# Splitting two weight matrices into high and low parts: POOL casts and VectorE subtracts, with a ring of four tiles

## The chip, the cores and the metric

The kernel runs on one core of a Trainium2 chip. A core has five engines that matter here: TensorE (PE, matrix products), VectorE (DVE), ScalarE (ACT), GpSimd (POOL) and SyncE (SP, which issues DMAs). Each takes its instructions in the order in which they are written, and they wait for each other by semaphores. The metric is the device time of one execution in microseconds, lower is better. Three runs before the change took 979.77, 981.46 and 983.20 us, median 981.46.

## The reference

The output is a block-causal attention followed by a gated MLP, all in float32:

```python
# q, k, v: (8 batches, 8 heads, 576 positions, 64 dims)
scores = (1 / sqrt(64)) * q @ k.T          # per batch and head
scores = where(block_i >= block_j, scores, -1e9)   # blocks of 64 positions
attn = softmax(scores)                     # with 1e-9 added to the sum
x = (attn @ v)                             # heads side by side: (4608, 512)
a = x @ w1                                 # (512, 1024)
b = x @ w2                                 # (512, 1024)
h = a * b @ w3                             # (1024, 1024)
out = h @ w_out                            # (1024, 512)
```

## The kernel before, in words

Two heads form a pair; the 8 batches have 4 pairs each, 32 in all. Pairs 0 to 3 (batch 0) are the early stage, the other 28 the long stage. In the long stage every pair's attention is interleaved with the MLP of the batch before. TensorE's order is written out by hand: `PLAN` and `EARLY_PLAN` (lines 46 to 62) list the steps of a pair as letters, S for a tile of scores, M for a step of the next pair's row maxima, V for a product with V, C for a step of weight preparation, W for a step of the product w3 @ w_out, which is computed once. The other engines' instructions are ordered by a scheduler that knows their dependencies; in the early stage the steps other than C and W have priority.

To keep float32 accuracy, the MLP multiplies split operands: w1 = w1h + w1l, w2 = w2h + w2l, where the high part is the value rounded to the type that TensorE takes in one pass (`fp32r`), and the low part is what is left. `gen_moe` uses w1h, w1l, w2h and w2l, `gen_prod` makes w3 @ w_out and splits it into `wh` and `wl`.

The weights arrive as raw 64-bit words. `load_w` (line 138) rebuilds one tile of 128x512 values, here called a unit, in five steps:

- SP loads the raw words into `wraw`, a ring of five buffers (L143).
- ScalarE writes the upper bits into `wy` (L150), a ring of buffers, and a byte of the lower bits into `wbits` (L151).
- POOL writes another byte into `wbits` (L152). There are two `wbits` tiles, used in turn.
- VectorE assembles `wy` and `wbits` to the value (L153): for w3 and w_out straight into their tiles `w3` and `wo`, for w1 and w2 back into `wy`.

For w1 and w2 `load_rows` (line 156) then writes the high part (L161) and the low part (L162) of each unit; a step C does two units, 16 units in all. A `wy` buffer is free again when the last reader of its value is done.

Around this, in the early stage: ScalarE's exp (`pe`, L273) takes each tile of scores (`s`, L265) from one of two buffers, and TensorE can't begin the next tile of scores until it has. VectorE's reductions (`m`, L196) take the row maxima out of the products `mx` (L192), also two buffers. Small DMAs on ScalarE's queue (L218, L232, L233) place the maxima (`ms`) and copies of Q and K into `qk`. L235 subtracts the high part of Q and K, L166 casts.

Of the kernel before, what the change touches and what calls it, by code (L numbers as in the profile page):

```python
# [8 lines left out]
F32 = mybir.dt.float32  # L9
# [6 lines left out]
ALU = mybir.AluOpType  # L16
# [3 lines left out]
P = 128  # L20
# [47 lines left out]
def block_causal_attention__then__gated_mlp_kernel(ctx, tc, qkv, consts, ident_in, w1, w2, w3t, wout, out_t):  # L68
    nc = tc.nc
# [47 lines left out]
    tl = {}  # L117
# [19 lines left out]

    def load_w(dst, src):
        t = tl["early"].tile([P, 1024], I32, tag="wraw", name="wraw", bufs=5)
        y = tl["early"].tile([P, 512], F32, tag="wy", name="wy", bufs=3)  # L140
        bits = tl["bits"][tl["unit"] % 2]
        tl["unit"] += 1
        nc.sync.dma_start(out=t, in_=src)  # L143
        high = t.rearrange("p (c two) -> p c two", two=2)[:, :, 1]
        byte = t.bitcast(U8).rearrange("p (c e) -> p c e", e=8)
        if dst is None:
            dst = y
        low = bits.bitcast(U8).rearrange("p (c e) -> p c e", e=4)[:, :, 0]
        top = bits.bitcast(F8).rearrange("p (c e) -> p c e", e=4)[:, :, 3]
        nc.scalar.mul(out=y, in_=high.bitcast(F32), mul=2.0**-112)  # L150
        nc.scalar.activation(out=top, in_=byte[:, :, 7], func=AF.Copy, bias=127.5 * 2.0**-60, scale=-(2.0**-60), saturate=False)  # L151
        nc.gpsimd.tensor_scalar(out=low, in0=byte[:, :, 3], scalar1=1.0 / 32, scalar2=-31.0 / 64, op0=ALU.mult, op1=ALU.add)  # L152
        nc.vector.scalar_tensor_tensor(out=dst.bitcast(I32), in0=y.bitcast(I32), scalar=3, in1=bits, op0=ALU.logical_shift_left, op1=ALU.bitwise_or)  # L153
        return y

    def load_rows(dst_h, dst_l, src):
        for c in range(NC):
            for h in range(2):
                cs = slice(h * 512, (h + 1) * 512)
                val = load_w(None, src[2 * c + h])  # L160
                nc.vector.tensor_copy(dst_h[:, c, cs], val)  # L161
                nc.gpsimd.tensor_tensor(out=dst_l[:, c, cs], in0=val, in1=dst_h[:, c, cs], op=ALU.subtract)  # L162
            yield

    def cast(n, dst, src, act):
# [208 lines left out]
    def gen_w(wp):  # L374
        def rows(u):
            for k in range(2 * u, 2 * u + 2):
                load_w(tl["wo"][:, k, :], wout[k])

        def w3(m):
            assert done[0] >= m - 1  # L380
            t3_of[m] = wp.tile([P, NF, P], F32, tag="w3", name="w3", bufs=2)
            for h in range(2):
                load_w(t3_of[m][:, 4 * h : 4 * h + 4, :].rearrange("p k f -> p (k f)"), w3t[2 * m + h])

        def split(dst_h, dst_l, src):
            g = load_rows(dst_h, dst_l, src)
            return lambda _: next(g)

        one, two = split(w1h, w1l, w1), split(w2h, w2l, w2)
        for u in range(4):  # L390
            rows(u)
            yield
        m, rest = 0, [one] * 4 + [two] * 4
        while m < NF or rest:
            if m < NF and done[0] >= m - 1 and (m < 2 or len(rest) <= 9 - m or not rest):
                w3(m)
                m += 1
            else:
                rest.pop(0)(None)
            yield  # L400
# [188 lines left out]
```

## Time and profile before

| what | value |
|---|---|
| median of three runs | 981.46 us (979.77 to 983.20) |
| the profiled execution | 982.55 us, span 980.6 us |
| PE busy | 941.6 us, 96% of the span |
| DVE busy | 692.4 us, 71% |
| ACT busy | 557.3 us, 57% |
| POOL busy | 629.6 us, 64% |
| mean granted clock of TensorE | 0.993 of full speed |

The span is from the first to the last instruction in the trace; the execution's own time is a little longer. The busy shares are means over the early and the long stage, so they have to be read stage by stage. In the rows below, `L162` is line 162 of the kernel, `w2l<-wy,w2h` says that w2l is written from wy and w2h, and a row of a timeline gives start, length, engine, line, operation, the number of instructions merged into it (`x2`) and, in brackets, how long the engine was idle before it and for whom it waited.

### The profile page before, as it was taken

The page shows a single profiled execution, that of the slowest core. Times are in us where ns is not written, and L with a number is a line of the kernel's source. Part 1 is how long each engine was busy: PE and PEld are TensorE (multiplying, and loading weights), DVE is VectorE, ACT ScalarE, POOL GpSimd, SP SyncE. Part 2 cuts the span into 40 slices and gives each one's busy share as a digit, 9 for nine tenths or more (in the row PEclk, how much of TensorE's full clock was granted, in tenths as well). Part 3 has the DMA queues.
Part 4 walks back from the last instruction along what each step waited for, and adds up shares of the span by engine and source line. Part 5 has one row for each costly group of instructions (what it writes and reads, how often), then busy time and mean ns, then how long its engine had stood idle before and what let it go on. Part 6 is the DMA issues. An engine that isn't in the chain of part 4 may idle for free.

```text
span 980.6 us, 18312 instructions
## 1 busy us (share of the span) xinstructions
PE 941.6 (96%) x6594; PEld 879.1 (90%) x6624; DVE 692.4 (71%) x1230; ACT 557.3 (57%) x1451; POOL 629.6 (64%) x605
## 2 busy tenths in 40 slices
PE   3788989999999999999999999999999999999998
PEld 1444449999999999999999999999999999999998
DVE  6776857777777778878777777788787877774100
ACT  6776635656556665566565556655656555553221
POOL 6786737767676767677676767676776767673211
PEclk9999989999999999999999999999999999999999
DMA  8967502222222221222222221211222222100000
GB/s 294 304 198 221 163 19 62 63 75 63 87 63 75 63 87 41 66 69 65 73 66 83 64 80 57 88 54 53 69 72 66 69 81 63 50 13 25 7 19 25
DMA packets 31303, 79.81 MB, mean 81 GB/s; under 512 B 5356, under 2 KB 13676, under 8 KB 31212
## 3 DMA queue, kind: packets, MB, share of 16 engines
q1 hardware_dynamic: 29788, 76.26, 25.4%
q10 hardware_dynamic: 1424, 2.38, 1.0%
q8 instruction: 52, 0.85, 0.4%
q14 instruction: 39, 0.32, 0.1%
HBM read 50.76 MB, written 9.44 MB: 61 GB/s over the span
## 4 chain that ended last, share of the span: by engine, by line
PE 88%; ACT 3%; DVE 3%; POOL 3%; issue 2%; DMA 1%; ACTq 0%; SPq 0%; POOLq 0%; DVEq 0%
PE ab L426 42%; PE o L442 21%; PE s L265 9%; PE x L320 9%; PE mx L192 3%; PE w L407 2%; POOL wbits L152 1%; ACT wbits L151 1%; DMA wraw<-in_w 1%; ACT wy L150 1%; POOL w2l L162 1%; PE x L304 1%; DVE m L196 1%; ACT pe L273 1%; DVE qk L166 0%
## 5 line engine op out<-in xcount | busy, mean ns | idle before, releaser
L286 POOL TENSOR_TENSOR rsum<-rsum,p 128x448 f32<-128x448 f32 x224 | 186.1, 831 | 87.1 <-ACT p L280 76.8
L435 POOL TENSOR_TENSOR gl<-g,gh 128x288 fp32r<-128x288 f32 x128 | 114.5, 895 | 121.5 <-ACT gh L434 121.5
L283 DVE TENSOR_TENSOR pl<-p,ph 128x448 fp32r<-128x448 f32 x168 | 149.1, 901 | 60.1 <-ACT ph L281 59.2
L265 PE MATMUL s<-qk 128*128 128x288 f32 (+4 forms) x768 | 157.3, 314 | 16.3 <-ACT pe L273 10.8
L235 POOL TENSOR_TENSOR qk<-raw,qk 64x1152 fp32r<-64x1152 f32 x58 | 154.9, 2670 | 9.1 <-issue 6.1
L426 PE MATMUL ab<-xh,w2h 128*128 128x288 f32 x512 | 153.8, 300 | 0.0
L442 PE MATMUL o<-gh,wh 128*128 128x288 f32 x512 | 153.6, 300 | 0.0
L426 PE MATMUL ab<-xh,w1h 128*128 128x288 f32 x512 | 151.1, 295 | 0.0
L426 PE MATMUL ab<-xl,w2h 128*128 128x288 f32 x512 | 151.0, 295 | 0.0
L426 PE MATMUL ab<-xl,w1h 128*128 128x288 f32 x512 | 151.0, 295 | 0.0
L426 PE MATMUL ab<-xh,w1l 128*128 128x288 f32 x512 | 151.0, 295 | 0.0
L442 PE MATMUL o<-gh,wl 128*128 128x288 f32 x512 | 150.9, 295 | 0.0
L426 PE MATMUL ab<-xh,w2l 128*128 128x288 f32 x512 | 150.9, 295 | 0.0
L442 PE MATMUL o<-gl,wh 128*128 128x288 f32 x512 | 150.8, 295 | 0.0
L265 PEld LDWEIGHTS s<-qk 128*128 128x128 f32 (+1 forms) x768 | 116.9, 183 | 28.5 <-ACT pe L273 16.1
L434 ACT CAST gh<-g 128x288 fp32r<-128x288 f32 x128 | 55.4, 433 | 142.8 <-DVE g L433 142.7
L281 ACT ACTIVATE ph<-s 128x288 fp32r<-128x288 f32 x336 | 131.4, 393 | 0.0
L196 DVE TENSOR_REDUCE m<-mx 128x1 f32<-128x64 f32 (+3 forms) x320 | 128.3, 446 | 3.0 <-PE mx L192 0.8
L280 ACT ACTIVATE p<-s 128x448 f32<-128x448 f32 x224 | 85.5, 382 | 51.5 <-PE s L265 50.7
L283 DVE TENSOR_TENSOR pl<-rsum,ph 128x288 fp32r<-128x288 f32 x112 | 75.7, 677 | 49.2 <-ACT ph L281 45.4
L320 PE MATMUL x<-ph,vs 128*128 128x128 f32 x336 | 110.4, 329 | 0.0
L433 DVE TENSOR_TENSOR g<-ab,a 128x288 f32<-128x288 f32 x128 | 56.5, 441 | 69.5 <-PE ab L426 68.6
(76 smaller groups left out, 2182.4 us busy)
## 6 DMA issues: line engine op xcount, KB each, us to landing
raw<-in_qkv SPq DMA_DIRECT2D x31, 896.0 KB
qk<-qk SPq DMA_DIRECT2D x108, 144.0 KB
out_t<-o SPq DMA_DIRECT2D x64, 144.0 KB
wraw<-in_w3t SPq DMA_DIRECT2D x16, 512.0 KB
wraw<-in_w SPq DMA_DIRECT2D x16, 512.0 KB
wraw<-in_wout SPq DMA_DIRECT2D x8, 512.0 KB
qk<-qk ACTq DMA_DIRECT2D x16, 144.0 KB
qk<-ms SPq DMA_DIRECT2D x54, 2.2 KB
```

Of the source, the lines that this page charges most:

```text
L196: nc.vector.reduce_max(m[:, col : col + 1], sc, axis=AX.X)
L235: (nc.gpsimd if "late" in tl or n * j else nc.vector).tensor_tensor(out=qk[j][o, 2:4], in0=rqk[o], in1=qk[j][o, 0:2], op=ALU.subtract)
L265: nc.tensor.matmul(t[ks, at : at + q1 - q0], qk[j][:, k, kr], qk[j][:, q, q0:q1], start=(s == 0), stop=(s == 1))
L280: nc.scalar.activation(p32, t[ks, at : at + w], AF.Exp, scale=SCALE)
L281: nc.scalar.activation(ph[ks, o : o + w], t[ks, at : at + w], AF.Exp, scale=SCALE)
L283: nc.vector.tensor_tensor(out=low, in0=p32, in1=ph[ks, o : o + w], op=ALU.subtract)
L286: nc.gpsimd.tensor_tensor(out=r, in0=r, in1=p32, op=ALU.add)
L320: nc.tensor.matmul(xps[:, to : to + w], v[:, c, :], pr[:, a : a + w], start=(u < 2 and s == 0), stop=(u in (0, len(PV) - 1) and s == len(p ...
L426: nc.tensor.matmul(t[:, 0:HALF], l[:, c, fs], r, start=(c == 0 and s == 0), stop=(c == NC - 1 and s == 2))
L433: nc.vector.tensor_tensor(out=g32, in0=acc[1][:, 0:HALF], in1=a32, op=ALU.mult)
L435: nc.gpsimd.tensor_tensor(out=gl[:, f, :], in0=g32, in1=gh[:, f, :], op=ALU.subtract)
L442: nc.tensor.matmul(t[:, 0:HALF], l[:, f, es], r[:, f, :], start=(f == 0 and s == 0), stop=(f == NF - 1 and s == 2))
```

## The change

POOL writes the high parts of w1 and w2 (L161) and VectorE the low parts (L162); before it was the reverse. The ring of `wy` has four buffers where it had three.

```diff
     def load_w(dst, src):
         t = tl["early"].tile([P, 1024], I32, tag="wraw", name="wraw", bufs=5)
-        y = tl["early"].tile([P, 512], F32, tag="wy", name="wy", bufs=3)
+        y = tl["early"].tile([P, 512], F32, tag="wy", name="wy", bufs=4)
...
                 val = load_w(None, src[2 * c + h])
-                nc.vector.tensor_copy(dst_h[:, c, cs], val)
-                nc.gpsimd.tensor_tensor(out=dst_l[:, c, cs], in0=val, in1=dst_h[:, c, cs], op=ALU.subtract)
+                nc.gpsimd.tensor_copy(dst_h[:, c, cs], val)
+                nc.vector.tensor_tensor(out=dst_l[:, c, cs], in0=val, in1=dst_h[:, c, cs], op=ALU.subtract)
```

The scheduler orders the engines anew; TensorE's order stays. Three places show how. Numbers behind a name tell tiles apart: `wy_932` and `wraw_931` belong to one unit, and units follow each other with rising numbers.

VectorE in pair 3, while the units 881 to 995 of w2 are made; before:

```order
L153 SCALAR_TENSOR_TENSOR wy_890<-wy_890,wbits1_110 128x512
L196 TENSOR_REDUCE m4_914<-mx4_1_926 128x1
L161 CAST w2h_88<-wy_890 128x512
L153 SCALAR_TENSOR_TENSOR wy_932<-wy_932,wbits0_109 128x512
L153 SCALAR_TENSOR_TENSOR wy_941<-wy_941,wbits1_110 128x512
L161 CAST w2h_88<-wy_932 128x512
L161 CAST w2h_88<-wy_941 128x512
L196 TENSOR_REDUCE m4_914<-mx4_2_956 128x1
L166 CAST qk0_86<-raw4_831 64x1152
L196 TENSOR_REDUCE m4_914<-mx4_2_956 128x1
L153 SCALAR_TENSOR_TENSOR wy_995<-wy_995,wbits0_109 128x512
```

The same stretch of VectorE after the change:

```order
L162 TENSOR_TENSOR w2l_89<-wy_890,w2h_88 128x512
L196 TENSOR_REDUCE m4_914<-mx4_1_926 128x1
L153 SCALAR_TENSOR_TENSOR wy_932<-wy_932,wbits0_109 128x512
L153 SCALAR_TENSOR_TENSOR wy_941<-wy_941,wbits1_110 128x512
L166 CAST qk0_86<-raw4_831 64x1152
L162 TENSOR_TENSOR w2l_89<-wy_932,w2h_88 128x512
L162 TENSOR_TENSOR w2l_89<-wy_941,w2h_88 128x512
L196 TENSOR_REDUCE m4_914<-mx4_2_956 128x1 x2
L153 SCALAR_TENSOR_TENSOR wy_995<-wy_995,wbits0_109 128x512
```

Both reductions of `mx4_2` now stand behind the subtractions of the units 932 and 941, and the cast of Q and K (L166) stands between those units' assemblies and their subtractions.

ScalarE at the end of pair 3's first head and the start of its second (`pe3_1`); before:

```order
L151 ACTIVATE wbits1_110<-wraw_1003 128x512
L150 ACTIVATE wy_1004<-wraw_1003 128x512
L232 DMA qk0_86<-qk0_86 64x576
L233 DMA qk0_86<-qk0_86 64x576
L150 ACTIVATE wy_1036<-wraw_1035 128x512
L151 ACTIVATE wbits0_109<-wraw_1035 128x512
L150 ACTIVATE wy_1043<-wraw_1042 128x512
L151 ACTIVATE wbits1_110<-wraw_1042 128x512
L273 ACTIVATE pe3_1_979<-s3_1_985 128x288
```

ScalarE there after the change:

```order
L151 ACTIVATE wbits1_110<-wraw_1003 128x512
L232 DMA qk0_86<-qk0_86 64x576
L233 DMA qk0_86<-qk0_86 64x576
L150 ACTIVATE wy_1036<-wraw_1035 128x512
L150 ACTIVATE wy_1043<-wraw_1042 128x512
L151 ACTIVATE wbits0_109<-wraw_1035 128x512
L151 ACTIVATE wbits1_110<-wraw_1042 128x512
L273 ACTIVATE pe3_1_979<-s3_1_985 128x288
```

`wy_1004` has moved further to the front, and the two `wy` of the units 1036 and 1043 stand together ahead of their `wbits`; the exp is still behind all four.

ScalarE at the same point of pair 2; before:

```order
L151 ACTIVATE wbits0_109<-wraw_793 128x512
L244 COPY ve0_154<-raw3_606 128x5x64
L150 ACTIVATE wy_801<-wraw_800 128x512
L273 ACTIVATE pe2_1_738<-s2_1_744 128x288
L273 ACTIVATE pe2_1_738<-s2_1_748 128x288
```

And after the change:

```order
L151 ACTIVATE wbits0_109<-wraw_793 128x512
L150 ACTIVATE wy_801<-wraw_800 128x512
L244 COPY ve0_154<-raw3_606 128x5x64
L273 ACTIVATE pe2_1_738<-s2_1_744 128x288
L273 ACTIVATE pe2_1_738<-s2_1_748 128x288
```

The copy of V (L244) and `wy_801` have changed places. Elsewhere POOL's order around these units is now cast, `wbits`, cast, `wbits`; on SP's queue the load of pair 4's Q, K and V stands ahead of one load of w2 that it followed before; on ScalarE's queue in pair 0 the DMA L232 stands behind two exps and two copies that followed it before; and in pair 2 one `wy` (unit 890) stands ahead of the DMA L218.

## Rows read from the trace of the kernel before

**Rows 1.** Busy time of each engine by stage (stretch: length, busy, instructions, clock, DMA).

```profile
20.00:149.30 129.30, 108.65 (x361) 58.35 (x365) 89.08 (x142) 82.74 (x166) 84.62 (x68) 0.95 0.58 180
...
149.30:980.60 831.30, 828.09 (x6220) 818.75 (x6245) 590.26 (x1068) 461.90 (x1266) 531.93 (x518) 1.00 0.21 61
```

**Rows 2.** Who waited for whom, 0 to 150 us (total us, times, longest).

```profile
PE s L265 <- ACT pe L273: 10.8, 8, 3.6
```

**Rows 3.** Lines 161, 162, 411, 0 to 150 us (ns minimum/median/maximum, start).

```profile
L161 DVE CAST w1h<-wy x8: 409/702/1383, 45.2 to 83.9; 128x512 fp32r<-128x512 f32 x8
...
L162 POOL TENSOR_TENSOR w2l<-wy,w2h x8: 1261/1581/2382, 90.5 to 125.8; 128x512 fp32r<-128x512 f32 x8
...
  ACT wy L150: 18.1, 12
...
L411 DVE TENSOR_TENSOR wl<-w,wh x8: 675/690/693, 52.1 to 149.6; 128x512 fp32r<-128x512 f32 x8
```

**Rows 4.** TensorE's timeline, 0 to 150 us.

```profile
43.60 0.63 PE L265 MATMUL s<-qk 128*128 128x288 f32 x3 [3.81 <-DMA qk<-ms]
...
59.88 0.68 PE L265 MATMUL s<-qk 128*128 128x448 f32 x2 [1.12 <-ACT pe L273]
...
63.74 0.56 PE L265 MATMUL s<-qk 128*128 128x192 f32 x4 [1.02 <-ACT pe L273]
...
69.23 0.95 PE L304 MATMUL x<-pe,ve 128*128 128x192 f32 x4 [0.76 <-ACT pe L273]
...
92.85 1.11 PE L265 MATMUL s<-qk 128*128 128x448 f32 x2 [3.00 <-ACT pe L273]
...
121.22 0.38 PE L192 MATMUL mx<-kb,qd 128*128 128x192 bf16 x2 [2.12 <-DVE m L196]
...
121.96 1.88 PE L407 MATMUL w<-wo,w 128*128 128x512 f32 x4
...
127.49 1.12 PE L265 MATMUL s<-qk 128*128 128x448 f32 x2 [3.65 <-ACT pe L273]
```

**Rows 5.** ScalarE's timeline, 0 to 150 us.

```profile
125.86 0.67 ACT L150 ACTIVATE wy<-wraw 128x512 f32<-128x512 f32 x1 [2.56 <-POOL w2l L162]
...
126.43 0.76 ACT L151 ACTIVATE wbits<-wraw 128x512 fp8e4<-128x512 uint8 x1
```

**Rows 6.** TensorE by slices of 2 us (length, busy, instructions, clock, DMA).

```profile
92.00:94.00 2.00, 1.15 (x5) 0.68 0.72 193
...
94.00:96.00 2.00, 2.00 (x6) 0.50 0.46 80
...
126.00:128.00 2.00, 0.51 (x1) 0.72 0.00 0
...
128.00:130.00 2.00, 2.00 (x7) 0.50 0.00 0
...
132.00:134.00 2.00, 2.00 (x7) 0.58 0.00 0
```

**Rows 7.** Groups of instructions, 0 to 160 us (count, busy us, mean ns, idle before).

```profile
L161 DVE CAST w2h<-wy 128x512 fp32r<-128x512 f32 x8 | 6.9, 882 | 0.0
...
L153 DVE SCALAR_TENSOR_TENSOR wy<-wy,wbits 128x512 int32<-128x512 int32 x16 | 13.9, 889 | 5.6 <-ACT wbits L151 5.5
...
L229 POOL CAST qk<-raw 64x576 fp32r<-64x576 f32 x1 | 0.7, 659 | 0.3 <-DMA raw<-in_qkv 0.3
...
L113 POOL CAST qk<-cst 64x576 fp32r<-64x576 f32 x4 | 4.6, 1147 | 1.9 <-DMA cst<-in_consts 1.7
```

**Rows 8.** VectorE's timeline, 0 to 150 us.

```profile
87.11 1.82 DVE L153 SCALAR_TENSOR_TENSOR wy<-wy,wbits 128x512 int32<-128x512 int32 x2
...
114.21 2.87 DVE L153 SCALAR_TENSOR_TENSOR wy<-wy,wbits 128x512 int32<-128x512 int32 x2
...
118.95 1.68 DVE L166 CAST qk<-raw 64x1152 fp32r<-64x1152 f32 x1
...
120.56 0.61 DVE L196 TENSOR_REDUCE m<-mx 128x1 f32<-128x448 f32 x1
```

## The prediction

> **What bounds the kernel now.** I read the span by stage first: up to 149.3 us the weights are prepared beside the first four pairs of heads, after it comes the long stage of attention and MLP. There TensorE is busy 828.09 of 831.30 us, so nothing that VectorE or POOL does there can be seen in the time; between 20 and 149.3 us it is busy 108.65 of 129.30 us, at a mean clock of 0.95 [rows 1]. Those 20.65 idle us, and what the lowered clock costs, are all that this change can reach (before 20 us no tile of w1 or w2 is handled).
>
> Next I read who waits there. TensorE's scores wait 10.8 us for ScalarE's exp. The exp waits for nothing of its own: ScalarE takes its work in order, and in that order stand the `wy` instructions (the first step of rebuilding a weight tile), which waited 18.1 us, 12 times, for POOL's subtractions of w1l and w2l [rows 2, 3]. A buffer of the `wy` ring is free when POOL has subtracted the tile three units back, and POOL needs a median 1.58 us for one [rows 3]. So the chain is: POOL's subtraction, ScalarE's `wy`, the exp queued behind it, TensorE.
>
> TensorE's timeline gives each such place its price [rows 4]. In pair 1: 1.12 us before the scores at 59.88, 1.02 at 63.74, 0.76 before the product with V at 69.23, together 2.90. In pair 2: 3.00 at 92.85. In pair 3: 2.12 at 121.22, where a reduction on VectorE is late, and 3.65 at 127.49. One more, 3.81 at 43.60, waits for a small DMA. ScalarE's timeline shows the last link before the longest: a `wy` at 125.86 after 2.56 us of waiting for POOL, and behind it `wbits` and the exp [rows 5].
>
> Both long gaps are also followed by a slow clock [rows 6]. Around 94 us the granted clock is 0.50 (1.2 GHz) where it was 1.00 (2.4 GHz) before the gap; half of the busy 1.15 and 2.00 us is lost, 1.6 us. After 126 us the busy 0.51, 2.00, 2.00 (two such slices, one shown) and 2.00 us at 0.58 lose 0.25 + 1.0 + 1.0 + 0.84 = 3.1 us. After the gap of 2.12 us alone the clock stayed at 1.00 (the matmuls that follow it took their usual time, and the 0.72 slice is the first low one).
>
> **The change part by part.**
>
> *POOL.* It loses 16 subtractions at a median of 1.58 us and gets 16 casts. POOL's casts in the trace are smaller: 64x576 in 0.659 us on the quick end, 1.147 us as a mean where VectorE works beside it [rows 7]. Scaled to 512 columns that is 0.59 to 1.02 us; I take 0.8, between the two. So POOL works about 16 x 0.8 = 12.5 us less. It is not on TensorE's path by itself, and this counts only through the waits above.
>
> *VectorE.* It loses 16 casts (mean 0.88 us for w2, 0.41 at best, 1.38 at worst) and gets 16 subtractions with both inputs in SBUF. The nearest rows: the subtraction of the same 128x512 with one input in the accumulators, 0.69; the 128x512 step with two tensor inputs that rebuilds the tile, mean 0.889 [rows 3, 7]. Lower end 0.68, upper end 0.69 plus the longest stretch that a cast suffered (1.38 - 0.41 = 0.97), 1.66. I take 0.89, the row of the same shape with two inputs: against a cast's 0.88 VectorE's load stays where it is.
>
> *The ring.* A `wy` now waits for the tile four units back, that is for the whole step before last, and its last reader is VectorE. In the order this reader stands ahead of the two assemblies of the next step, so ScalarE's `wy` no longer ends the chain. What is late next is `wbits`, which has two buffers as before and waits for VectorE's assembly two units back.
>
> *The added wait.* Each VectorE subtraction waits for POOL's cast of the same tile. Behind it on VectorE stand the row-maximum reductions that free the buffers of TensorE's `mx` products. Mostly the scheduler has put reductions or casts between an assembly and its subtraction, and POOL's order is cast, `wbits`, cast, `wbits`, so one POOL instruction of 0.8 to 1.0 us lies between.
>
> *Moves without a price.* In pair 0 one DMA (L232) on ScalarE's queue goes behind two exps and two copies, about 2 us, while its scores at 43.60 wait for a later one. On SP's queue the load of pair 4's Q, K and V passes one w2 tile; if that cover failed, the tile's two steps would be late by that one load. Reductions and exps in pair 0 move by one `wy`, worth up to 0.6 us, but the wait at 43.60 is for a DMA behind them, so I count none.
>
> Now the places, in the times of before.
> Pair 1: all three gaps were exps behind a `wy` that waited for POOL. The order leaves only waits on assemblies, which were done by then: 2.90 falls to 0.4, saving 2.5.
> Pair 2: the exp behind the gap now waits for `wbits`, that is for two assemblies on VectorE that ended by 88.9 [rows 8], then one `wy` (0.67) and a copy of V: about 90. 3.00 falls to 0.5, saving 2.5, and the clock stays up, 1.6.
> Pair 3, first gap: before, VectorE needed from 114.21 to 121.17 for two assemblies (2.87 with a wait for ScalarE in them), two casts, a cast of Q and K (1.68) and two reductions [rows 8]. After, the same stretch is 2 x 0.89 + 1.68 + 2 x 0.89 + 0.8 = 6.0, ending at 120.2 instead of 121.17: saving 0.9.
> Pair 3, second gap: after that reduction come two assemblies (to 122.0); from the start of the last `wbits` at 126.43 to the scores at 127.49 it took 1.1 us before, so TensorE resumes at 123.1 to 123.2; the four matmuls in front (1.88 us from 121.96, now 0.9 earlier) end at 122.9. Resuming at 123.2 instead of 127.49 saves 4.3, of which 0.9 is already counted, so 3.4; and the clock, 3.1.
> Together 2.5 + 2.5 + 1.6 + 0.9 + 3.4 + 3.1 = 14.0. Against it: one `wy` (0.67, counted 0.6) now stands ahead of the small DMA for the scores of pair 3, whose twin in pair 1 was waited for at 43.60, and I allow 0.9, one subtraction's length, for those that wait for a cast in pair 2. That leaves 12.5. The profiled execution took 982.55, so 970.05; it lay 1.09 above the median of the runs shown, which by itself would give 969.0. I forecast 969.5.
>
> One rule speaks against the exchange. The row: the subtraction with one input in the accumulators always took 0.675 to 0.693, while casts in SBUF went from 0.41 to 1.38 [rows 3]. The Trainium skill, "SBUF — State Buffer", section "Who interferes with whom", says that a VectorE instruction with two SBUF inputs contends with a GpSimd instruction that reads SBUF, and that the loser blocks for the other's whole length. The rows agree; by it every new subtraction can be held by a whole POOL instruction, as the casts were. That is the slow rival below.
>
> **The rivals.**
> 1. *One long gap remains.* The `wbits` ring of two makes ScalarE wait for VectorE, and if subtractions take 1.2 us rather than 0.89, four of them in pair 3 bring the first gap back to 2.4 and leave the clock to fall once. Then the 3.1 and about 2.4 more are not gained: 12.5 - 5.5 = 7.0, 975.5. For it: from 114.21 to 121.17 VectorE goes from one row to the next almost without idle time [rows 8]. Against it: over 20 to 149.3 us it works 89.08 of 129.30 [rows 1], and its load does not grow.
> 2. *The wait only changes its place.* ScalarE's 18.1 us become VectorE's waits for casts, and the reductions are late by as much as the exps were. 14.0 spread over the seven steps of w1 and w2 that lie beside the gaps (of eight) is 2.0 us a step; with that much added on VectorE nothing is gained: 981. Against it: POOL has 12.5 us more time.
> 3. *Slower.* Each subtraction is held by a POOL instruction (1.66 - 0.88 = 0.78, twice a step), and each first subtraction waits for a cast behind a `wbits` (1.0 + 1.02 less the second assembly 0.89, so about 1.1, and 0.4 for the second): 3.1 a step, seven steps, 21.7 against 14.0 saved: 7.7 slower, 990. It decides from 2.0 us a step on. For it: the rule above, and VectorE's order is fixed. Against it: the scheduler put other work between, and casts are half as long as subtractions on POOL.
>
> **How the numbers follow.** Forecast 0.63 (its own range 965 to 973), rival 1 0.20 (975.5), rival 2 0.10 (981), rival 3 0.07 (990). 0.3% of 981.46 is 2.9 us, about what a measurement of this kernel can tell from no change: faster means under 978.5. That gives 0.83 faster, 0.10 the same, 0.07 slower. The range 964 to 979 takes in the forecast and rival 1, and leaves the other two and gains above 17 us outside.
>
> **What would show it.** Right: in the profile after, `wy` waits for the subtraction's line for less than 3 us in total; the gaps of 3.00 and 3.65 are under 1 us; the granted clock is 1.00 in the slices after them; VectorE's subtractions have a mean near 0.9 and POOL's casts near 0.8; the long stage begins near 137 and still takes 831 us. Wrong: subtractions above 1.3, VectorE's reductions waiting behind casts with TensorE's `mx` products late by more than 2 us, a clock of 0.50 after 60 us, or a new long wait for the small DMA in front of the scores.

## The result, and the profile after

The changed kernel takes 970.76 us (median of 6 runs, 968.63 to 974.43), against 981.42 for the kernel before (6 runs). The ratio is 0.9888, with a 95% interval of 0.9869 to 0.9908: 10.7 us faster, and 1.3 us above the forecast of 969.5. Run again with the last experiments, it gave 971.94 and 0.9903 (0.9878 to 0.9927).

The profiled execution took 970.15 us, its span is 968.3 us. The view of busy time by stage, with the border moved to where the long stage now begins (length, busy time of PE, PEld, DVE, ACT, POOL, clock, DMA share, GB/s), answers to [rows 1]:

```profile
20.00:137.15 117.15, 105.90 (x364) 57.88 (x365) 89.81 (x142) 81.35 (x165) 72.57 (x68) 0.97 0.64 198
137.15:968.30 831.15, 828.00 (x6247) 818.75 (x6245) 589.45 (x1068) 461.86 (x1266) 531.56 (x518) 1.00 0.21 61
```

The long stage is what it was, 831.15 us after 831.30. The early stage is 12.15 us shorter; VectorE's load there hardly moved (89.81 after 89.08), POOL's fell by 12.05.

Who waited for whom, 0 to 150 us, all engines (total us, times, longest), answers to [rows 2] and to the waits of `wy` in [rows 3]:

```profile
PE s L265 <- ACT pe L273: 3.6, 5, 1.4
...
ACT wy L150 <- DVE w2l L162: 2.8, 4, 1.5
...
DVE w2l L162 <- POOL w2h L161: 2.7, 2, 1.3
...
DVE w1l L162 <- POOL w1h L161: 1.0, 2, 0.5
ACT wy L150 <- DVE w1l L162: 1.0, 1, 1.0
```

The first step `wy` waited 18.1 us for POOL's subtractions and now waits 3.8 for VectorE's, in 5 places where there were 12; the prediction had asked for less than 3. TensorE's waits for an exp fell from 10.8 us to 3.6. The price, VectorE waiting for POOL's casts, is 3.7 us.

The exchanged operations by line (minimum/median/maximum ns, start), again for [rows 3], and their means (last number before the second bar):

```profile
L161 POOL CAST w1h<-wy x8: 609/947/1022, 43.8 to 82.8; 128x512 fp32r<-128x512 f32 x8
...
L162 DVE TENSOR_TENSOR w1l<-wy,w1h x8: 674/693/1183, 44.9 to 84.3; 128x512 fp32r<-128x512 f32 x8
L162 DVE TENSOR_TENSOR w2l<-wy,w2h x8: 675/685/983, 89.2 to 120.4; 128x512 fp32r<-128x512 f32 x8
```

```profile
L161 POOL CAST w1h<-wy 128x512 fp32r<-128x512 f32 x8 | 6.8, 848 | 6.0 <-DVE wy L153 5.8
L161 POOL CAST w2h<-wy 128x512 fp32r<-128x512 f32 x8 | 6.5, 809 | 2.8 <-DVE wy L153 2.6
L162 DVE TENSOR_TENSOR w1l<-wy,w1h 128x512 fp32r<-128x512 f32 x8 | 6.2, 796 | 1.0 <-POOL w1h L161 1.0
L162 DVE TENSOR_TENSOR w2l<-wy,w2h 128x512 fp32r<-128x512 f32 x8 | 5.9, 757 | 2.7 <-POOL w2h L161 2.7
```

TensorE's timeline, for [rows 4] (start, us, engine, line, operation, and in brackets the idle time before it with its releaser):

```profile
45.78 0.61 PE L192 MATMUL mx<-kb,qd 128*128 128x512 bf16 x1 [2.07 <-ACT qd L166]
...
55.88 0.80 PE L265 MATMUL s<-qk 128*128 128x288 f32 x4
...
71.61 1.09 PE L265 MATMUL s<-qk 128*128 128x288 f32 x4
...
75.88 0.96 PE L265 MATMUL s<-qk 128*128 128x448 f32 x4 [1.24 <-ACT pe L273]
...
88.28 0.67 PE L265 MATMUL s<-qk 128*128 128x448 f32 x2
...
103.28 0.66 PE L265 MATMUL s<-qk 128*128 128x288 f32 x3 [1.05 <-DMA qk<-ms]
...
115.96 0.38 PE L192 MATMUL mx<-kb,qd 128*128 128x192 bf16 x2 [2.02 <-DVE m L196]
...
118.25 0.74 PE L265 MATMUL s<-qk 128*128 128x448 f32 x2
...
136.24 1.09 PE L265 MATMUL s<-qk 128*128 128x288 f32 x4
```

The scores at 88.28 and 118.25 are those that stood behind gaps of 3.00 and 3.65 us; they now follow the work in front of them at once. New are the gaps of 2.07 at 45.78 and of 1.24 at 75.88; the scores that had waited 3.81 us for the small DMA (43.60) now wait 0.45 us, at 41.35. To see where the time came from I set the same instructions of both timelines side by side:

| instruction | before | after | shift | step of the prediction, forecast and found |
|---|---|---|---|---|
| scores, pair 1, second head | 56.23 | 55.88 | -0.35 | none forecast |
| first scores, pair 2 | 74.97 | 71.61 | -3.36 | pair 1: 2.5 saved, found 3.0 |
| product with V, pair 2, first head | 85.23 | 83.60 | -1.63 | new gap and others: 0.9 lost, found 1.7 |
| first scores, pair 3 | 107.18 | 101.54 | -5.64 | pair 2, gap and clock: 4.1 saved, found 4.0 |
| product with V, pair 3, first head | 117.45 | 112.55 | -4.90 | small DMA: 0.6 lost, found 0.7 |
| scores, pair 3, second head | 121.33 | 116.06 | -5.27 | first gap: 0.9 saved, found 0.4 |
| first scores of the long stage | 148.39 | 136.24 | -12.15 | second gap and clock: 6.5 saved, found 6.9 |

The granted clock after the two places, for [rows 6] (slices of 2 us, same columns as above):

```profile
116.00:118.00 2.00, 2.00 (x10) 1.27 (x9) 1.97 (x5) 1.47 (x3) 1.35 (x2) 1.00 0.00 0
118.00:120.00 2.00, 2.00 (x10) 1.19 (x9) 1.97 (x5) 1.88 (x5) 1.81 (x3) 1.00 0.00 0
```

It is at its upper level (1.00, 2.4 GHz), as in every such slice from 50 to 140 us of this execution. (In the repeated run it was not: the last section shows a fall to 0.50 near 116 us.)

### The profile page after: what moved, and what is told of

It reads as the page before. It is cut to its first block, busy times and chain, and to the rows that moved or that the text cites. A ratio compares the mean times of both kernels' runs of the same rounds, so it can differ in the third digit from the quotient of the medians.

```text
span 968.3 us, 18335 instructions
## 1 busy us (share of the span) xinstructions
PE 938.8 (97%) x6624; PEld 878.7 (91%) x6624; DVE 692.3 (72%) x1230; ACT 556.6 (57%) x1451; POOL 617.5 (64%) x605
## 4 chain that ended last, share of the span: by engine, by line
PE 89%; ACT 3%; DVE 3%; POOL 2%; issue 1%; DMA 1%; ACTq 0%; SPq 0%; DVEq 0%; POOLq 0%
PE ab L426 42%; PE o L442 21%; PE s L265 9%; PE x L320 9%; PE mx L192 4%; PE w L407 2%; POOL wbits L152 1%; ACT wbits L151 1%; ACT wy L150 1%; PE x L304 1%; DVE m L196 1%; ACT pe L273 1%; DMA qk<-ms 1%; DVE w L153 0%; PE tot L337 0%
## 5 line engine op out<-in xcount | busy, mean ns | idle before, releaser
L265 PE MATMUL s<-qk 128*128 128x288 f32 (+4 forms) x768 | 155.2, 311 | 6.1 <-ACT pe L273 3.6
L235 POOL TENSOR_TENSOR qk<-raw,qk 64x1152 fp32r<-64x1152 f32 x58 | 155.0, 2673 | 8.6 <-issue 5.6
```

The source lines that it names most:

```text
L235: (nc.gpsimd if "late" in tl or n * j else nc.vector).tensor_tensor(out=qk[j][o, 2:4], in0=rqk[o], in1=qk[j][o, 0:2], op=ALU.subtract)
L265: nc.tensor.matmul(t[ks, at : at + q1 - q0], qk[j][:, k, kr], qk[j][:, q, q0:q1], start=(s == 0), stop=(s == 1))
```

## The experiments

Medians, ratios to the kernel before with their 95% intervals, and, from each profile, where the long stage begins and how long `wy` waited for the subtractions. The experiments ran on three chips, the kernel before beside them on each, so the ratios compare better than the medians:

| kernel | median us | ratio | long stage begins | `wy` waited |
|---|---|---|---|---|
| before | 981.3 to 981.7 | 1 | 148.39 | 18.1 |
| after | 970.76 | 0.9888 (0.9869 to 0.9908) | 136.24 | 3.8 |
| after, again | 971.94 | 0.9903 (0.9878 to 0.9927) | 136.49 | 5.0 |
| engines exchanged, ring of three | 970.84 | 0.9895 (0.9872 to 0.9918) | 136.56 | 3.7 |
| ring of four, engines as before | 979.53 | 0.9975 (0.9962 to 0.9988) | 145.25 | 8.5 |
| exps repeated, 6 times | 973.14 | 0.9911 (0.9891 to 0.9930) | 137.51 | 3.9 |
| exps repeated, 14 times | 974.88 | 0.9938 (0.9915 to 0.9962) | 140.54 | 4.1 |
| one long hold of ScalarE | 977.30 | 0.9961 (0.9948 to 0.9973) | 141.37 | 5.0 |
| casts on VectorE too | 970.71 | 0.9905 (0.9890 to 0.9921) | 133.86 | 3.7 |
| L235 on VectorE | 968.20 | 0.9871 (0.9857 to 0.9885) | 135.18 | 4.2 |
| subtractions put later | 970.15 | 0.9886 (0.9873 to 0.9900) | 134.47 | 3.7 |
| L358 on VectorE | 968.86 | 0.9875 (0.9850 to 0.9901) | 134.67 | 5.0 |
| later, and L235 on VectorE | 968.21 | 0.9863 (0.9840 to 0.9886) | 132.70 | 4.4 |
| all three edits | 965.55 | 0.9840 (0.9819 to 0.9861) | 131.90 | 4.4 |

**Which half of the change does it.** Theory A takes the wait for a buffer whose last reader was POOL's subtraction as the cause and gives each half of the change a part of the gain; Theory B puts it all on POOL's shorter work.

```diff
 # swap_only: the exchange without the fourth buffer
-        y = tl["early"].tile([P, 512], F32, tag="wy", name="wy", bufs=4)
+        y = tl["early"].tile([P, 512], F32, tag="wy", name="wy", bufs=3)
```

> The two engines exchanged as in the change, the ring of wy left at three buffers. Theory A (the time went into ScalarE's wait for a buffer whose last reader was POOL's slow subtraction, and each half of the change shortens that wait): wy still waits for the tile three units back, now for a chain of cast and subtraction that spans two engines, so about half of the 18 us of waiting stays and at least one of the two gaps of more than 3 us in pairs 2 and 3 stays: 974 to 978. Theory B (POOL's 12.5 us less work is what counts): the same time as with the whole change, 970 to 972.

```diff
 # ring_only: four buffers, the engines as in the kernel before
-                nc.gpsimd.tensor_copy(dst_h[:, c, cs], val)
-                nc.vector.tensor_tensor(out=dst_l[:, c, cs], in0=val, in1=dst_h[:, c, cs], op=ALU.subtract)
+                nc.vector.tensor_copy(dst_h[:, c, cs], val)
+                nc.gpsimd.tensor_tensor(out=dst_l[:, c, cs], in0=val, in1=dst_h[:, c, cs], op=ALU.subtract)
```

> The ring of wy with four buffers, casts on VectorE and subtractions on POOL as before. Theory A: wy waits for the step before last, whose subtractions POOL has mostly done; ScalarE's wait for POOL falls from 18 to under 6 us, the gap of 3.65 in pair 3 shrinks below 2: 971 to 975. Theory B (POOL's work is what counts): POOL is as late as before and the tiles come no earlier: 979 to 982.

Theory A's ranges missed both times and Theory B's held (970.84 and 979.53). The exchange alone gives the whole gain, as far as the intervals can tell; the ring alone gives 2.0 us. The waits of the kernel with only the longer ring:

```profile
PE s L265 <- ACT pe L273: 9.4, 6, 2.4
...
ACT wy L150 <- POOL w2l L162: 5.3, 3, 2.3
...
ACT wy L150 <- POOL w1l L162: 3.2, 3, 1.6
```

A fourth buffer halves what `wy` waits for POOL (8.5 us of 18.1), but TensorE still waits 9.4 us for exps after 10.8. Two of its four gaps over 1.5 us there stand behind a `wy` that waited for POOL's subtraction (1.59 and 2.27 us); the other two stand behind other links, POOL's product L358 (2.23 us) and VectorE's transposes (3.08 us). With the subtraction on VectorE three buffers wait as little as four (3.7 and 3.8 us). The exchange does two things at once: it puts the buffer's last reader on an engine that does it in less than half the time, and it takes some 12 us of work off POOL; no run parts the two.

**What a gap costs beyond its length.** The forecast took 4.7 us of its sum from the granted clock. These kernels put a hold of ScalarE back into the changed kernel, in front of the exps of pair 3's second head, where the gap of 3.65 had been.

```diff
 # gap_short: 6 repeats; gap_long: 14
-                nc.scalar.activation(p_early[ks, o : o + w], t[ks, at : at + w], AF.Exp, scale=SCALE)
+                for _ in range(6 if n == 3 and j == 1 and c == 0 and q0 == 0 else 1):
+                    nc.scalar.activation(p_early[ks, o : o + w], t[ks, at : at + w], AF.Exp, scale=SCALE)
```

> The changed kernel, in which the first exp of pair 3's second head is done six times over the same data (same values): ScalarE is held for five more exps of about 0.3 us there, 1.5 us. Theory: TensorE waits 1.5 us longer in front of the next scores, the granted clock stays at 1.00 behind the gap, and the time is 1.5 us above the changed kernel: 972.3. Rival (the clock falls after any such gap): 1.5 plus about 3: 975.3.

> The same with fourteen times: thirteen more exps, 3.9 us. Theory: the gap is as long as the one before the change (3.65), the clock falls to 1.2 GHz behind it and some 3 us more are lost: 970.8 + 3.9 + 3 = 977.7. Rival (the slow clock before the change had another cause than that gap): only 3.9: 974.7.

Both failed as tests of the clock, though 974.88 is near the rival's number. The scheduler spread the repeats among other work, and gaps of 1.95 us (6 repeats), and of 1.95 and 1.57 (14), came out; behind them the clock stayed at 1.00. From the first scores of pair 3's second head to the long stage these kernels took 2.4 and 4.3 us longer than the changed kernel, of which the gaps are 1.95 and 3.52; the rest was not traced. The next kernel made one gap:

```diff
 # gap_single: ahead of the true exps, written over by them
+        if n == 3 and j == 1 and todo[0][0] == 0 and todo[0][3] == 0:
+            for _ in range(3):
+                nc.scalar.activation(p_early[:, 0:1440].rearrange("p (a b) -> p a b", b=288),
+                    t[:, 0:288].unsqueeze(1).broadcast_to([P, 5, 288]), AF.Exp, scale=SCALE)
```

> The changed kernel with ScalarE held some 3.6 us in one piece, by three extra exponentials that write 1440 columns each before the first true ones of pair 3's second head (the values are written again after them), so that TensorE has one gap behind `pe` there, of the kind and place that the kernel before had (3.65 us at 127.49). Theory A (the gap costs its own length, and the low granted clock after it as much again): a gap of 3 to 4 us near 119 to 122, granted clock near 0.5 to 0.7 in the slices after it, 976 to 978. Theory B (the low clock of the kernel before had another cause than the length of the gap): the same gap, clock at 1.00 after it, 973 to 975.

Its gap on TensorE, and the slices behind it:

```profile
122.05 1.11 PE L265 MATMUL s<-qk 128*128 128x448 f32 x2 [2.98 <-ACT pe L276]
```

```profile
122.00:124.00 2.00, 1.95 (x7) 1.53 (x8) 1.48 (x4) 1.10 (x4) 0.00 (x0) 0.50 0.00 0
124.00:126.00 2.00, 2.00 (x5) 0.84 (x4) 0.12 (x2) 1.86 (x4) 0.00 (x0) 0.74 0.03 8
```

Theory A held in time (977.3) and in kind: the clock fell to 0.50. The repeated run of the changed kernel is its control, with the same gap of 3.1 us before it near 115 (114.56, and 114.84 with the hold) and the same low clock after that. From there the kernel with the hold loses (141.37 - 136.49) - (114.84 - 114.56) = 4.6 us: 2.98 is the gap, 1.95 x 0.5 + 2.00 x 0.26 = 1.5 the clock, 0.1 is left. So in this execution the clock added half of the gap's length to its price, not as much again.

**Is POOL still the bound?**

```diff
 # all_dve: POOL neither casts nor subtracts
-                nc.gpsimd.tensor_copy(dst_h[:, c, cs], val)
+                nc.vector.tensor_copy(dst_h[:, c, cs], val)
```

> The changed kernel with the casts of w1 and w2 on VectorE as well as the subtractions: POOL does neither (its 16 casts, 13.3 us between 20 and 138 us of the changed kernel, fall away), VectorE gets both (72.2 + 12.5 us of other work and these, some 103 of the stage's 118 us). Theory A (the time hung on the work that POOL had in front of ScalarE's next first step; whatever takes it off POOL does as well): no exponential waits over 1.5 us, the gap of 2.02 us at 115.96 that the late cast on POOL made goes as well, 968.5 to 970.5. Theory B (VectorE is by now as near the path as POOL was): the maxima and assembled tiles come later by half of the 12.5 us added, gaps of TensorE behind VectorE's `m` and `w` over 1.5 us in pairs 1 to 3, 974 to 979.

Neither theory's range holds 970.71, and Theory A's is missed by little. VectorE's load rose by 6.6 us, not by the 12.5 that the expectation had taken. The time is that of the changed kernel, with VectorE's work up from 90.35 to 96.99 us between 20 and 138 us and POOL's down from 72.70 to 61.87. Theory A expected the gap behind `m` to go with the late casts. It did not, and a gap of this kind is what Theory B had named:

```profile
113.40 0.38 PE L192 MATMUL mx<-kb,qd 128*128 128x192 bf16 x2 [2.00 <-DVE m L196]
```

So that gap is not POOL's alone: with the casts on VectorE, VectorE's own work in front of the reductions, without a wait in it from 104.00 us on, fills the same 2 us. Its profiled execution was its quickest (967.84 of 967.84 to 973.82), with the clock at 1.00 in every slice from 28 us on; its early start of the long stage is partly that.

**The new gap of 1.24 us in pair 2.** VectorE's assemblies of `w` in the changed kernel by line (minimum/median/maximum ns), VectorE's timeline, then POOL's, where it begins:

```profile
L153 DVE SCALAR_TENSOR_TENSOR w<-wy,wbits x16: 674/683/3112, 27.8 to 122.6; 128x512 int32<-128x512 int32 x16
```

```profile
65.41 4.23 DVE L153 SCALAR_TENSOR_TENSOR w<-wy,wbits 128x512 int32<-128x512 int32 x2
...
70.27 0.78 DVE L344 STREAM_TRANSPOSE tr<-x 64x576 f32<-64x576 f32 x1
```

```profile
66.20 2.88 POOL L235 TENSOR_TENSOR qk<-raw,qk 64x1152 fp32r<-64x1152 f32 x1
...
72.51 1.40 POOL L358 TENSOR_TENSOR x<-x,rb 128x576 f32<-128x576 f32 x1 [1.40 <-DVE rb L357]
```

The second assembly of a `w` took 3112 ns, 0.68 us being usual, and ended 0.56 us after POOL's subtraction L235 (65.41 + 4.23 and 66.20 + 2.88). Behind it on VectorE wait the transposes of pair 1's row sums, then POOL's product of x and the reciprocal row sums (L358), then ScalarE's rounding of it to `xh`, and behind that, in ScalarE's order, the exp. Two edits take one link each:

```diff
 # dve235: the second heads' low parts of Q and K on VectorE
-        (nc.gpsimd if "late" in tl or n * j else nc.vector).tensor_tensor(out=qk[j][o, 2:4], in0=rqk[o], in1=qk[j][o, 0:2], op=ALU.subtract)
+        (nc.gpsimd if "late" in tl else nc.vector).tensor_tensor(out=qk[j][o, 2:4], in0=rqk[o], in1=qk[j][o, 0:2], op=ALU.subtract)
```

> The changed kernel with the subtraction of the second heads' low parts of q and k (L235, 64x1152) on VectorE in pairs 1 to 3 as well, as it is for the first heads already; on POOL it took 2.74 us each. Theory A (the new gap of 1.24 us at 75.88 came because VectorE's assembly of a `w` was held 3.1 us beside POOL's 2.88 us of this subtraction): no assembly over 1.5 us, that gap under 0.4 us, 968 to 969.7. Theory B (the gap came from the length of ScalarE's queue, the held assembly only lay beside it): gap of 1 us or more still there, 970 to 972, since VectorE gets 1.5 us more in each pair.

```diff
 # x358: the product with the reciprocal row sums on VectorE in all pairs
-        (nc.gpsimd if n < 2 else nc.vector).tensor_tensor(out=x32, in0=x32, in1=rb, op=ALU.mult)
+        nc.vector.tensor_tensor(out=x32, in0=x32, in1=rb, op=ALU.mult)
```

> The changed kernel with the product of x and the reciprocal row sums (L358, 128x576) on VectorE for pairs 0 and 1 too; on POOL it took 1.40 us each, for the later pairs VectorE does it in 0.76. Theory A (the gap of 1.24 us at 75.88 stands at the end of the chain `rb` on VectorE, x on POOL, `xh` on ScalarE, then `pe`; ScalarE waits 2.23 us before `xh` and holds all exponentials behind it): the wait before `xh` about 0.7 us shorter in both pairs, that gap 0.4 to 0.7 us, in all 969 to 970. Theory B (the gap is the held assembly of `w` on VectorE, 3.1 us): gap still 1.1 us or more, 970 to 971.5.

The same scores in the repeated run, with L235 moved, and with L358 moved:

```profile
74.30 0.96 PE L265 MATMUL s<-qk 128*128 128x448 f32 x4 [1.95 <-ACT pe L273]
```

```profile
73.58 0.96 PE L265 MATMUL s<-qk 128*128 128x448 f32 x4 [1.12 <-ACT pe L273]
```

```profile
72.84 0.95 PE L265 MATMUL s<-qk 128*128 128x448 f32 x4 [1.26 <-ACT pe L273]
```

The repeated run shows that the gap was 1.95 in another execution; TensorE had come there 2.3 us earlier. Against it each edit takes about 0.7 to 0.8. L235 on VectorE: the held assembly is gone (0.69 and 0.88 at this place, none over 1.09), but the 1.74 us that VectorE now works on L235 stand in its place, and only 0.8 is gained here. L358 on VectorE: ScalarE's wait before `xh` falls from 2.23 to 1.55. So the held assembly and the chain to `xh` are both links, and neither edit ends the gap: Theory A failed on the gap's size in both runs (under 0.4, and 0.4 to 0.7), and Theory B's gaps stood (1.12 and 1.26); of the times, 968.20 lies in Theory A's range and 968.86 just below it. Neither kernel's interval is clear of the changed kernel's.

**The gap behind `m` in pair 3.**

```diff
 # defer: a step's subtractions are issued at the start of the next step
-                nc.vector.tensor_tensor(out=dst_l[:, c, cs], in0=val, in1=dst_h[:, c, cs], op=ALU.subtract)
+                late_sub.append((dst_l[:, c, cs], val, dst_h[:, c, cs]))
...
         while m < NF or rest:
+            flush()        # issues what late_sub holds
...
+        flush()
```

> The changed kernel with the subtractions of a step on w1 and w2 put at the start of the next step, so that VectorE's maxima stand ahead of them and no longer wait for POOL's cast. Theory A (the gap of 2.02 us at 115.96, behind `m`, stayed because VectorE stood 1.33 us before a subtraction for POOL's cast): that gap under 1 us, VectorE's waits for a cast near 0 (3.7 us in the changed kernel), 968.5 to 970. Theory B (the gap has the length of the score matmuls and reductions themselves; the wait only lay in it): still 1.5 us or more there, 970 to 971.5.

The gap of 2.02 us at 115.96 is gone (no gap over 0.9 us between 103 and 140 us), VectorE's waits for casts fell from 3.7 to 1.5 us, and the long stage began 1.8 us earlier. But the span is the same 968.3: a gap of 1.95 us stayed at 74.74, and the long stage shows two new waits for the small DMA in front of scores, 1.2 us together; where the other 0.6 went was not traced. By itself the edit is worth nothing that can be told from none.

**Together.** The repeated run of the changed kernel was the measure:

> The changed kernel itself once more, as the measure for the three that are built on it. Both theories: 969.5 to 971.5, gaps of TensorE at the same places (2.0 us behind `m` near 116, 1.2 us or more behind `pe` near 75). What differs is what the low granted clock does between executions: if it follows from the order of the program, it stands in the same slices (32 to 36 and 46 to 50 us) as before; if not, it stands elsewhere or is missing, with a span shorter by 1.5 to 2 us for each place that is missing.

It lies just above its range (971.94), its gaps are longer than expected (3.11 behind `m`, 1.95 behind `pe`), and its low clock stands in other slices; its span is no shorter for that (968.5 after 968.3).

> Both single edits together: the subtractions of a step at the start of the next one, and the second heads' low parts (L235) on VectorE. Theory A (they act at different places: L235 between 36 and 60 us, where `wbits` no longer lies 2.9 us behind it on POOL; the late subtractions at the gap of 2.02 us behind `m` near 116): the gaps near 116 under 1 us, the long stage begins near 133 to 134, 966 to 967.5. Theory B (the subtractions put later are given back as waits of the next first step, as in the run with the late subtractions alone, whose long stage began 1.8 us earlier and ended no earlier): 968 to 970.

> The three edits together: late subtractions, L235 and L358 on VectorE. VectorE gets some 4.6 + 1.5 us more than in the changed kernel, POOL 11 us less. Theory A (what ends the gaps is POOL's place in the chains to the exponentials): no gap behind `pe` over 1 us after 40 us, 965 to 966.8. Theory B (VectorE, by now with some 96 us of work in the stage's 118, ends them): gaps behind `m` or `w` of 1.5 us or more in pairs 1 to 3, 968 or more.

The two edits together gave 968.21, which is Theory B's range, though the places went as Theory A said (1.15 us behind `m`, the long stage from 132.70) and `wy` waited no longer than before (4.4 us after 5.0), so nothing shows the giving back that B stood for. The executions went from 966.52, the profiled one, to 969.89. All three gave 965.55, in Theory A's range, and the interval of the ratio, 0.9819 to 0.9861, lies clear of the changed kernel's. TensorE's gaps between 60 us and the long stage that are over 0.4 us:

```profile
72.43 0.97 PE L272 MATMUL s<-qk 128*128 128x448 f32 x4 [0.42 <-ACT pe L280]
...
84.90 0.67 PE L272 MATMUL s<-qk 128*128 128x448 f32 x2 [0.79 <-ACT pe L280]
...
110.50 0.38 PE L199 MATMUL mx<-kb,qd 128*128 128x192 bf16 x2 [1.15 <-DVE m L203]
...
113.97 0.68 PE L272 MATMUL s<-qk 128*128 128x448 f32 x2 [0.85 <-ACT pe L280]
```

The gap at the end of the chain in pair 2 has the size that the two single edits would leave of it (1.95 - 0.83 - 0.69 = 0.43, measured 0.42), but that they add up so closely is partly chance: with L235 moved and the subtractions put later it was 0.65 already, not 1.12. This is the version that beats both kernels, 16 us under the kernel before.

## Why the prediction was right

*The chain.* POOL's subtraction, ScalarE's `wy`, the exp behind it, TensorE: right. When the engines alone were exchanged, the whole gain came; whether by the quicker last reader or by POOL's lighter load was not parted.

*The ring.* This step named the right effect and gave two reasons for it, that `wy` "now waits for the tile four units back" and that its last reader is on VectorE. Only the second was needed: with three buffers `wy` waited as little. The forecast needed no split, so the sum was not hurt, but a reader who had kept only the ring would have got 2.0 us.

*Durations.* Casts on POOL: 0.8 taken, means 0.848 and 0.809. (The 12.5 us less for POOL are 16 times 1.58 - 0.8, not 16 x 0.8 as the prediction has it; found 12.05.) Subtractions on VectorE: 0.89 taken, means 0.796 and 0.757, medians 0.69. The nearer row was not the assembly of the same shape but the subtraction with one input in the accumulators, the lower bound; that VectorE's load stayed came out right.

*Pairs 1 and 2.* The gaps went as forecast (the table of shifts), and the clock after the one at 92.85 with it. The 0.9 allowed in pair 2 for subtractions that wait was too small and had another cause: 1.7 us were lost, 1.24 of them in the gap behind the held assembly, which the prediction had not seen.

*Pair 3, first gap.* This step of the prediction failed. It forecast 2.12 to 1.2 by counting VectorE's instructions end to end; the gap is 2.02, and 3.11 in the second execution. That is also the prediction's own sign of being wrong, `mx` products late by more than 2 us behind reductions that wait for casts. The step left out the wait that "the added wait" itself describes. VectorE's and POOL's rows after:

```profile
112.54 0.68 DVE L162 TENSOR_TENSOR w2l<-wy,w2h 128x512 fp32r<-128x512 f32 x1
114.54 0.69 DVE L162 TENSOR_TENSOR w2l<-wy,w2h 128x512 fp32r<-128x512 f32 x1 [1.33 <-POOL w2h L161]
115.15 0.75 DVE L196 TENSOR_REDUCE m<-mx 128x1 f32<-128x64 f32 x2
```

```profile
111.00 1.01 POOL L161 CAST w2h<-wy 128x512 fp32r<-128x512 f32 x1 [0.63 <-DVE wy L153]
112.08 1.76 POOL L152 TENSOR_SCALAR wbits<-wraw 128x512 uint8<-128x512 uint8 x1
113.90 0.61 POOL L161 CAST w2h<-wy 128x512 fp32r<-128x512 f32 x1
```

Between two casts lies one `wbits`, not of 0.8 to 1.0 us but of 1.76, with VectorE at work beside it (its shortest in this stage took 0.76; that VectorE lengthened this one is likely, and was not tried). The second subtraction stands 1.33 us, and the reductions behind it. The kernel with the late subtractions removed this gap, which shows the wait for the cast as the cause in that order of the work; with the casts on VectorE its own work took the wait's place.

*Pair 3, second gap, and the clock.* 6.5 forecast, 6.9 found. That the low clock was part of the price is shown in kind, by one execution: a gap made there brought it back. Its size is not settled: 1.5 us behind a gap of 2.98, while the 3.1 for the gap of 3.65 was read from the slices of before. And the forecast that the clock stays up held in one of the two profiled executions only: the repeated run shows 0.50 at 116 us, behind the first gap, which is another of the prediction's signs of being wrong.

*The rivals.* Of the one that only changes the place of the wait, 3.7 of 18.1 us came true. The slow one asked for subtractions held by 0.78 us each; the longest took 1.183, and medians stayed at 0.69. A hold of that kind did show once, on another instruction: the assembly of 3112 ns lay beside POOL's 2.88 us and ended just after it, and with L235 off POOL it was gone. By the Trainium skill, "SBUF — State Buffer", section "Who interferes with whom", a VectorE instruction with two SBUF inputs contends with a GpSimd instruction that reads SBUF, and the one that comes second waits for the whole of the other. The trace agrees there; for the exchanged subtractions, no row shows a hold of a whole POOL instruction. The casts that the prediction took to agree with the rule have one SBUF input, not two, and were no test of it.

*The sum.* Profile against profile the step from 982.55 to 970.15 is 12.40 us, 12.5 forecast. The medians differ by 10.7, because the profiled execution of before lay 1.1 above its median and that of after 0.6 below. That the sum came out so closely is partly luck. Its misses are up to 0.8 us and of both signs (the table of shifts), and the stretch around 43.60, where the prediction counted nothing ("Moves without a price"), moved by more than the table shows. The scores behind the small DMA came 1.9 to 2.3 us earlier (43.60 before, 41.35, and 41.67 in the repeated run). In the first execution the gap of 2.07 us at 45.78 and the low clock behind it gave most of that back; in the repeated run it lasted to the scores of the second head in pair 1 (54.30 after 56.23) and was given back in pair 3, by the gap of 3.11 and the low clock behind that one. Why these scores came earlier was not traced.

## What to carry to other kernels

When a queue in program order stands between a slow helper and the bound engine, shorten the helper's work before lengthening the ring: here the first was worth 10.7 us, the second 2.0 alone and nothing that can be told from none on top. Once a bound is gone, the next gaps are chains of several engines, and single edits at one link gave at most some 3 us, none clear of the changed kernel's interval, while three together gave 5 to 6 and were clear of it: test them together before throwing one away. And where an instruction is given a wait for another engine, count that engine's instructions in between at the length they have beside a busy neighbour, not at their quick one (here 1.76 us, not 0.8 to 1.0).

## What was not expected of the hardware

The granted clock does not follow from a gap's length alone. In the changed kernel's first execution it fell to 0.50 after a gap of 2.07 us at 45.78 and stayed at 1.00 after one of 2.02 at 115.96:

```profile
46.00:48.00 2.00, 2.00 (x7) 1.53 (x7) 1.40 (x3) 1.94 (x4) 1.86 (x2) 0.50 0.56 219
48.00:50.00 2.00, 2.00 (x6) 0.95 (x4) 0.69 (x1) 1.87 (x4) 0.00 (x0) 0.71 0.84 236
```

In the repeated run of the same program these slices are at 1.00, and the clock fell near 115 instead, after 3.11 us:

```profile
114.00:116.00 2.00, 1.45 (x7) 1.38 (x7) 2.00 (x5) 1.42 (x3) 1.30 (x2) 0.73 0.01 4
116.00:118.00 2.00, 2.00 (x3) 0.67 (x2) 1.94 (x5) 1.72 (x4) 1.78 (x4) 0.50 0.00 0
```

With the casts on VectorE, gaps of 3.32 us at 43.16 and 2.00 at 113.40 were followed by 1.00. Shorter gaps show both as well. In the changed kernel's first execution the clock was low behind one of 1.40 us:

```profile
31.77 0.64 PE L265 MATMUL s<-qk 128*128 128x192 f32 x4 [1.40 <-ACT pe L273]
```

```profile
32.00:34.00 2.00, 2.00 (x8) 0.52 0.98 365
34.00:36.00 2.00, 2.00 (x5) 0.63 1.06 269
```

There the low clock cost little, because a wait stood behind it: the scores that wait for the small DMA came at 41.35, and at 41.67 in the repeated run, where these slices are at 1.00 and the wait was 2.17 us in place of 0.45. With L358 moved the scores of 31.77 stood behind a gap of 1.41 us, and the clock stayed at 1.00. So between 1.4 and 3.3 us the runs show both, and one program shows them in different places from one execution to the next; this may be a part of what spreads its times over 968.6 to 976.1 us. What decides it in an execution stays open. And the two executions reached the long stage within 0.25 us of each other (136.24 and 136.49): when TensorE is held up early by a low clock, it finds a later gap shorter (2.02 us for 3.11 near 115), as it would if the engines that make it have gone on meanwhile; that was not tried by itself.
